# A list-scheduled attention and two-layer feed-forward kernel: new cost constants for the planner, other places for the weight rounding, six copies per pass on another engine

## The chip, the core and the metric

The kernel runs on one core of a Trainium2 chip. The metric is the device time of one execution in microseconds (us). The engines are TensorE (PE; its weight loads are shown as PEld), VectorE (DVE), ScalarE (ACT), GpSimd (POOL) and SyncE (SP, which issues most DMAs). Each engine works through its own instructions in program order, and waits for others by semaphores.

## The reference

Attention with 4 batches, 12 heads, 448 tokens and heads of 64; then two feed-forward layers on the 1792 tokens of width 768:

```python
scores = cap * np.tanh(np.matmul(q, k.transpose(0, 1, 3, 2)) * scale / cap)
attn = np.exp(scores - np.max(scores, axis=-1, keepdims=True))
attn = attn / (np.sum(attn, axis=-1, keepdims=True) + 1e-09)
x = np.matmul(attn, v)                    # then laid out as (1792, 768)
x = np.maximum(x @ w_in, 0.0) ** 2 @ w_out      # w_in 768x2048, w_out 2048x768
x = np.maximum(x @ w_in2, 0.0) ** 2 @ w_out2
```

## The kernel before

**Arithmetic.** The two feed-forward layers are computed by Strassen-Winograd products: seven products named A11, A12, S3, S2, S1, S4 and A22 instead of eight. Every fp32 operand is split into a high part (a copy to the matmul's format) and a low part (the operand minus the high part, always on VectorE), and a product takes three matmuls: high by high, high by low, low by high (lines 632 to 634).

**Stages.** Attention runs over 24 pairs of heads (`pair`). The feed-forward work runs in four passes, two for each layer, each for two batches (`layer`, `bring`, `blocks_of_g`, `stream`). A pass streams 56 chunks of weights: a chunk is six 128x128 tiles, and PE needs 18 matmuls for it. In the first 28 chunks of a pass the first product of the layer (w_in) is done, in the last 28 the second (w_out), while `blocks_of_g` makes and splits sums of the activations.

**Work on VectorE and ScalarE.** For each chunk ScalarE makes the high part of the weights (`wh`, line 284) and VectorE the low part (`wl`, line 200 through the helper `minus`; line 203 is the helper `sub`). At the start of a pass `bring` loads the twelve tiles of x of that pass, and `split_x` makes the parts of seven combinations for each of three columns c: the high part by ScalarE (line 449) or by VectorE (line 451), as its last argument says, and the low part by VectorE. Before the change S2 and A22 take VectorE, the five others ScalarE.

**Rounding of words.** The weights arrive as 64-bit words. `round_words` turns a word block into fp32: a load on SP, one ScalarE scale (line 230), three VectorE instructions (lines 233, 236, 239), and a store to DRAM on POOL's queue (line 242). `round_block` does two of them and then four sums on GpSimd (line 267), stored too. A layer has 17 blocks (8 of w_in, 9 of w_out). The buffers are few: two for words once the early blocks are done, three for the results (`wg`), a result's buffer being given back when its sums are stored.

**What sets the order.** All is written as operations with an engine, an estimated cost in ns, a place (a due time in chunks) and dependences, and `Plan.emit` orders them by a list schedule: each engine keeps a clock that the estimated costs advance. Of the first 40 waiting operations of an engine, none more than 6 places ahead of PE's next one, it takes the first that can start at the engine's clock, or else the one that can start earliest; the engine that can start first of all goes next. So the costs, the places and the engines decide the order in which each engine's queue is written; on the chip the queues then run in that order, at their own speed. `act(n)` and `dve(n, rate)` give the costs, `place` and `t0` the places. `START` is place 60.8, where pass 0 begins, and pass p begins 56 p places later.

Of the kernel before, what the change touches and what calls it, by code (L numbers as in the profile page):

```python
# [15 lines left out]
B, H, S, D = 4, 12, 448, 64  # L16
# [3 lines left out]
QW = 960  # L20
# [8 lines left out]
START = 24 * PAIR + 2  # L29
# [4 lines left out]
class Plan:  # L34
# [12 lines left out]
    def op(self, engine, cost, emit, place, deps=(), take=(), drop=(), after=()):  # L47


        self.ops.append([engine, cost, emit, place, list(deps), list(take), list(drop), None, list(after)])  # L50
        return len(self.ops) - 1
# [103 lines left out]
def pipeline(ctx: ExitStack, tc: tile.TileContext, qk, v, capt, rcap, eps, win, wout, w32, sums, x1, x2, out):  # L155
# [35 lines left out]
    op = plan.op  # L191

    def act(n, psum=False):
        return 0.833 * n + (145 if psum else 93)

    def dve(n, rate=1.04):
        return rate * n + 67

    def minus(out, a, b):
        nc.vector.tensor_tensor(out, a, b.bitcast(F32), op=ALU.subtract)  # L200
# [10 lines left out]
    def round_words(l, u, t0, ring, early):  # L211


        g, i, k = UNITS[u]
        c0, c1 = FP[k] if g else (0, HC)
        nk = 2 * (c1 - c0)
        n = nk * 128
        words = next(turns) % (3 if early else 2)
        m = {"at": [None]}

        def load():
            m["t"] = w_8[words]
            src = (wout[l][i] if g else win[l][i]).bitcast(U32).rearrange("p (h c) -> p h c", h=2)[:, :, c0 * 256:c1 * 256]
            nc.sync.dma_start(m["t"][:, :n].rearrange("p (h m) w -> p h (m w)", h=2), src)

        def scale():
            m["f"] = w_g[m["at"][0]]
            m["ff"] = m["f"].rearrange("p c m -> p (c m)")[:, :n]
            m["fu"] = m["ff"].bitcast(U32)
            nc.scalar.activation(m["ff"], m["t"][:, :n, 1].bitcast(F32), AF.Copy, scale=2.0 ** -112)  # L230

        def shift():
            nc.vector.tensor_scalar(m["fu"], m["fu"], 3, 1, op0=ALU.logical_shift_left, op1=ALU.bitwise_or)

        def lower():
            nc.vector.scalar_tensor_tensor(m["fu"], m["t"][:, :n, 0], 29, m["fu"], op0=ALU.logical_shift_right, op1=ALU.bitwise_or)  # L236

        def sign():
            nc.vector.scalar_tensor_tensor(m["fu"], m["t"][:, :n, 1], 0x80000000, m["fu"], op0=ALU.bitwise_and, op1=ALU.bitwise_or)

        def store():
            nc.gpsimd.dma_start(w32[l, g, i][:, :, c0:c1], m["f"][:, :nk].rearrange("p (h c) m -> p h c m", h=2))

        o = op("SP", n * 1024, load, t0 - 2, take=[f"ww{words}"])
        o = op("ACT", act(n), scale, t0, [o], take=[(ring, m["at"])])
        o = op("DVE", dve(n, 0.52), shift, t0, [o])
        o = op("DVE", dve(n), lower, t0, [o])
        o = op("DVE", dve(n), sign, t0, [o], drop=[f"ww{words}"])
        if words == 2:
            guard.update({(0, "c", f): [o] for f in range(4)})  # L250
        stored[l, u] = op("POOL", n * 512, store, t0, [o])
        return m

    def round_block(l, g, i, k, t0, early):


        c0, c1 = (0, HC) if g == 0 else FP[k]
        n = c1 - c0
        us = [unit_of(g, r, k) for r in (i, i + (HF if g == 0 else HC))]
        ring = "wx" if early and (i + k) % 2 == 0 else "wg"  # L260
        ms = [round_words(l, u, t0 + 2.2 * r, ring, early) for r, u in enumerate(us)]

        def one_sum(q):
            a11, a12, a21, a22 = (m["f"][:, h * n:h * n + n] for m in ms for h in range(2))
            out, a, b, how = [(a22, a21, a22, ALU.add), (a21, a11, a21, ALU.subtract),
                              (a11, a22, a11, ALU.subtract), (a12, a12, a11, ALU.subtract)][q]
            nc.gpsimd.tensor_tensor(out, a, b, op=how)  # L267

        def store():
            for r, m in enumerate(ms):  # L270
                nc.gpsimd.dma_start(sums[l, g, i][:, 2 * r:2 * r + 2, c0:c1], m["f"][:, :2 * n].rearrange("p (h c) m -> p h c m", h=2))

        o = [stored[l, u] for u in us]
        for q in range(4):
            o = [op("GP", dve(n * 128, 2.9), lambda q=q: one_sum(q), t0 + 4.5, o)]
        summed[l, g, i, k] = op("POOL", 4 * n * 128 * 512, store, t0 + 4.5, o, drop=[(ring, m["at"]) for m in ms])
        if ring == "wx":
            guard.update({(0, "d", f): [summed[l, g, i, k]] for f in range(HF)})
# [20 lines left out]
    def pair(b, j, t0, step):  # L299


        stk, pv, m = {}, {}, {}
# [23 lines left out]
        t = t0 - 3 * step  # L326
        o = op("SP", 128 * QW * 4, load_qk, t - 4, take=["raw"])
        o = op("DVE", dve(QW, 0.6), hi, t, [o], take=["qkh"])
        parts = op("DVE", dve(QW), lo, t, [o], take=["qkl"], drop=["raw"])
        v_ready = op("SP", 128 * VL * 4, load_v, t0 - 4.5, take=["vr"])  # L330

        banks = [("pv", [None]) for _ in range(2)]
        done = None
        for gi, tiles in enumerate(GROUPS):
            s, n = {"at": [None]}, len(tiles) * S
# [51 lines left out]
        def den(a):  # L387
            if a == 0:
                m["d"] = sp.tile([128, S], F32, tag="d", name="d")
            rows, of = (slice(0, 64), slice(64, 128)) if a == 0 else (slice(64, 128), slice(0, 64))  # L390
            nc.scalar.activation(m["d"][rows], pv["AB"[a]][of, :S], AF.Identity, bias=eps[of])  # L391
# [11 lines left out]
        t1 = t0 + dt[3] + 3 * step  # L403
        to = {B * NP - 2: "XY", B * NP - 1: "XZ"}.get(nth)
        back = [(to[e] if to else "pv", banks[e][1]) for e in range(2)]
        o = op("ACT", act(S), lambda: den(0), t1, [done], take=["d"])
        o = op("ACT", act(S), lambda: den(1), t1, [o])
        o = op("DVE", dve(S, 6.25), rec, t1, [o])
        o = op("DVE", dve(S), lambda: mul(0), t1, [o], drop=back[:1])
        o = op("DVE", dve(S), lambda: mul(1), t1, [o], drop=back[1:])  # L410
# [32 lines left out]
    def split_x(src, name, c, p, place, deps, on_act):  # L443

        cell = [None]

        def hi():
            if on_act:
                nc.scalar.activation(slots[cell[0]][:, 0], src(), AF.Copy)
            else:  # L450
                nc.vector.tensor_copy(slots[cell[0]][:, 0], src())

        def lo():
            minus(slots[cell[0]][:, 1], src(), slots[cell[0]][:, 0])

        o = op("ACT" if on_act else "DVE", act(S) if on_act else dve(S, 0.52), hi, place, deps, take=[("x", cell)])
        o = op("DVE", dve(S), lo, place, [o])
        x_set[p, name, c] = cell, o
        return o
# [3 lines left out]
    def bring(p, c, spots, place, t_in, free):  # L463

        l, b1 = p // 2, 2 * (p % 2)
        b2 = b1 + 1
        m = {}
        cells = [(b1, c), (b2, c), (b1, c + HC), (b2, c + HC)]

        def load():  # L470
            m["t"] = [two[n][:, i] for n, i in spots]
            for q, (b, i) in enumerate(cells):
                nc.sync.dma_start(m["t"][q], (x2 if l else x1)[b, i])

        def t2():
            m["d"] = sp.tile([128, S], F32, tag="d", name="t2") if p else two["c"][:, 5 + c]
            sub(m["d"], m["t"][3], m["t"][0])

        ring = ["d"] if p else []
        ld = op("SP", 4 * 128 * S * 4, load, t_in, [*(stored_x[l, b, i] for b, i in cells), *free])  # L480
        o1 = split_x(lambda: m["t"][0], "A11", c, p, place("A11", c), [ld], True)
        o2 = split_x(lambda: m["t"][2], "A12", c, p, place("A12", c), [ld], True)
        o = op("DVE", dve(S), lambda: sub(m["t"][0], m["t"][1], m["t"][0]), place("S3", c) - 0.2, [o1])
        o3 = op("DVE", dve(S), lambda: sub(m["t"][1], m["t"][3], m["t"][1]), place("S3", c) - 0.1, [o])
        split_x(lambda: m["t"][1], "S3", c, p, place("S3", c), [o3], True)
        o4 = op("DVE", dve(S), t2, place("S2", c) - 0.1, [o3], take=ring)
        o6 = split_x(lambda: m["d"], "S2", c, p, place("S2", c), [o4], False)
        o5 = op("DVE", dve(S), lambda: sub(m["t"][2], m["t"][2], m["d"]), place("S2", c) + 0.1, [o6, o2], drop=ring)
        o7 = split_x(lambda: m["t"][0], "S1", c, p, place("S1", c), [o], True)
        o8 = split_x(lambda: m["t"][3], "S4", c, p, place("S4", c), [ld], True)  # L490
        last = split_x(lambda: m["t"][2], "A22", c, p, place("A22", c), [o5, o7, o8], False)
        guard.update({(p, *spot): [last] for spot in [*spots, *([] if p else [("c", 5 + c)])]})

    def split_g(p, name, q, src, place, deps):
# [229 lines left out]

    blocks = [(g, f, 0) for g in range(1) for f in range(HF)] + [(1, i, k) for i in range(HC) for k in range(3)]
    for q, block in enumerate(blocks):
        round_block(0, *block, 2 + 4.7 * q, q < 11)
    for q, block in enumerate(blocks):
        round_block(1, *block, START + 32+6.4 * q, False)
    for n in range(B * NP):  # L730
        pair(*divmod(n, NP), PAIR * n, 0.65)
    op("PE", 0, open_two, START - 0.5, ready_x[-1:], drop=[("x", [NX + i]) for i in range(NY)])
# [140 lines left out]
```

## Time and profile before

| what | value |
|---|---|
| median of three runs | 1124.91 us (1124.22 to 1127.05) |
| the profiled execution | 1121.83 us, its span 1120.0 us |
| mean granted TensorE clock | 0.986 |
| PE busy, 4920 matmuls | 94% |
| DVE busy, 976 instructions | 77% |
| ACT busy, 1119 instructions | 68% |
| POOL busy, 324 instructions | 25% |

How to read it: matmuls are pipelined, so a busy PE is not PE at its peak; the number of matmuls that start in a stretch tells more. The shares are means over stages with different limits, and are read stage by stage below.

### The profile page before, as it was taken

To read this page: it belongs to the slowest core of one execution; us is meant where nothing else is said; L and a number is where in the kernel's file an instruction comes from. 1 tells how busy PE (TensorE), PEld (TensorE's weight loads), DVE (VectorE), ACT (ScalarE), POOL (GpSimd) and SP (SyncE) were. 2 spreads that over 40 slices of the span, in tenths; PEclk is the share of its full clock that TensorE was granted. 3 is DMA by queue.
4 is the path that set the end of the run, shared out by engine and by line. 5 is a ranking of instruction groups with operands and counts; after the bars stand their busy time and mean duration, and the time that the engine had idled before them with its cause. 6 is when DMAs were issued, how large, how long until landed. Compare 5 with 4: busy or idle time off the path is not lost.

```text
span 1120.0 us, 14647 instructions
## 1 busy us (share of the span) xinstructions
PE 1054.1 (94%) x4920; PEld 869.4 (78%) x4920; DVE 861.8 (77%) x976; ACT 763.3 (68%) x1119; POOL 284.0 (25%) x324
## 2 busy tenths in 40 slices
PE   6999998986999998989999889899999999999997
PEld 3444444445999897889988778799999989999996
DVE  4999898999567998985589989755886863367851
ACT  6999999884778565557775655577765556686541
POOL 0354353423223505332433333324200000000000
PEclk9999999888999999999999999999999999999999
DMA  9889899753777668767876687776446443333441
GB/s 265 295 275 314 263 292 335 238 190 116 273 231 235 224 203 295 242 239 242 279 226 209 208 312 244 224 237 227 157 138 211 152 135 99 114 100 120 131 145 58
DMA packets 107684, 237.79 MB, mean 212 GB/s; under 512 B 13648, under 2 KB 62032, under 8 KB 107600
## 3 DMA queue, kind: packets, MB, share of 16 engines
q1 hardware_dynamic: 92112, 175.42, 51.0%
q0 software_dynamic: 15488, 61.35, 14.7%
q8 instruction: 40, 0.66, 0.2%
q14 instruction: 44, 0.36, 0.1%
HBM read 169.87 MB, written 66.85 MB: 211 GB/s over the span
## 4 chain that ended last, share of the span: by engine, by line
PE 55%; DVE 14%; ACT 11%; issue 9%; DMA 6%; POOL 4%; SPq 0%; DVEq 0%; ACTq 0%; POOLq 0%
PE bank L634 16%; PE bank L632 16%; PE bank L633 16%; PE bank L362 4%; ACT bank L350 4%; DVE wl L200 3%; POOL wg L267 3%; ACT pe L354 2%; PE bank L345 2%; ACT d L391 2%; DVE xb L200 2%; DVE xc L200 2%; DMA wo<-wg 2%; DVE d L394 2%; DVE wg L236 1%
## 5 line engine op out<-in xcount | busy, mean ns | idle before, releaser
L200 DVE TENSOR_TENSOR wl<-wf,wh 128x768 fp32r<-128x768 f32 x224 | 226.7, 1014 | 147.9 <-ACT wh L284 147.3
L634 PE MATMUL bank<-xc,wl 128*128 128x448 f32 x756 | 278.9, 369 | 11.0 <-DVE wl L200 10.9
L632 PE MATMUL bank<-xc,wh 128*128 128x448 f32 x756 | 278.5, 368 | 8.8 <-ACT bank L650 3.7
L284 ACT ACTIVATE wh<-wf 128x768 fp32r<-128x768 f32 x224 | 187.7, 840 | 137.5 <-PE bank L633 105.2
L633 PE MATMUL bank<-xc,wh 128*128 128x448 f32 x762 | 280.1, 368 | 1.2 <-DVE xc L200 1.0
L632 PE MATMUL bank<-xb,wh 128*128 128x448 f32 x588 | 216.1, 368 | 7.1 <-ACT wh L284 2.4
L634 PE MATMUL bank<-xb,wl 128*128 128x448 f32 x588 | 215.5, 367 | 3.3 <-DVE wl L200 3.3
L633 PE MATMUL bank<-xb,wh 128*128 128x448 f32 x582 | 213.1, 366 | 1.7 <-DVE xb L200 1.7
L634 PEld LDWEIGHTS bank<-xc,wl 128*128 128x128 f32 x756 | 142.9, 189 | 25.9 <-DVE wl L200 14.3
L632 PEld LDWEIGHTS bank<-xc,wh 128*128 128x128 f32 x756 | 142.8, 189 | 23.5 <-ACT bank L650 4.9
L362 PE MATMUL bank<-pe,vr 128*128 128x448 f32 (+1 forms) x384 | 155.2, 586 | 1.4 <-DVE d L398 1.1
L633 PEld LDWEIGHTS bank<-xc,wh 128*128 128x128 f32 x762 | 144.0, 189 | 13.8 <-DVE xc L200 2.1
L632 PEld LDWEIGHTS bank<-xb,wh 128*128 128x128 f32 x588 | 110.7, 188 | 19.4 <-ACT wh L284 3.2
L634 PEld LDWEIGHTS bank<-xb,wl 128*128 128x128 f32 x588 | 110.6, 188 | 13.8 <-DVE wl L200 4.8
L633 PEld LDWEIGHTS bank<-xb,wh 128*128 128x128 f32 x582 | 109.6, 188 | 10.9 <-DVE xb L200 2.1
L362 PEld LDWEIGHTS bank<-pe,vr 128*128 128x128 f32 (+1 forms) x384 | 59.1, 194 | 67.7 <-issue 36.3
L350 ACT ACTIVATE bank<-bank,caps 128x896 f32<-128x896 f32 x96 | 84.2, 877 | 18.6 <-PE bank L345 18.6
L267 POOL TENSOR_TENSOR wg<-wg 128x384 f32<-128x384 f32 (+1 forms) x56 | 76.4, 1365 | 60.7 <-DMA wo<-wg 46.0
L354 ACT ACTIVATE pe<-bank,caps 128x896 f32<-128x896 f32 x96 | 87.8, 914 | 3.1
L658 ACT ACTIVATE one<-bank 128x448 f32<-128x448 f32 x88 | 47.1, 536 | 49.5 <-PE bank L634 37.0
L345 PE MATMUL bank<-qkh 64*128 64x448 f32 (+1 forms) x168 | 56.7, 573 | 23.1 <-ACT pe L354 16.4
L676 DVE TENSOR_TENSOR one<-bank,one 128x448 f32<-128x448 f32 x64 | 39.7, 620 | 44.6 <-PE bank L634 35.6
(116 smaller groups left out, 1381.9 us busy)
## 6 DMA issues: line engine op xcount, KB each, us to landing
wf<-si SPq DMA_DIRECT2D x120, 192.0 KB, 3.0
ww<-win_dram SPq DMA_DIRECT2D x27, 768.0 KB, 6.7
wf<-wi SPq DMA_DIRECT2D x96, 192.0 KB, 3.2
ww<-wout_dram SPq DMA_DIRECT2D x23, 768.0 KB, 6.5
wf<-so SPq DMA_DIRECT2D x32, 384.0 KB, 3.7
raw<-qk_dram SPq DMA_DIRECT2D x48, 240.0 KB, 5.2
wi<-wg POOLq DMA_DIRECT2D x24, 384.0 KB, 5.8
si<-wg POOLq DMA_DIRECT2D x24, 384.0 KB, 4.3
```

What stands on the lines that cost most here:

```text
L200: nc.vector.tensor_tensor(out, a, b.bitcast(F32), op=ALU.subtract)
L267: nc.gpsimd.tensor_tensor(out, a, b, op=how)
L284: nc.scalar.activation(m["hi"], m["f"], AF.Copy)
L345: nc.tensor.matmul(s["s"][:, i, :S], lhsT=k[rows, S + 128 * t:S + 128 * t + 128], rhs=q[rows, :S], start=k_low + q_low == 0, stop=k_low == 1)
L350: nc.scalar.activation(s["s"], s["s"], AF.Tanh, scale=rcap)
L354: nc.scalar.activation(s["p"][:, :k], s["s"], AF.Exp, scale=capt)
L362: nc.tensor.matmul(pv[a][:, :S], lhsT=m["v"][rows, w:w + 128], rhs=s["p"][rows, i], start=t == 0, stop=t == 3)
L632: nc.tensor.matmul(a, lhsT=hi, rhs=x(0), start=first and z == 0, stop=False, skip_group_check=more)
L633: nc.tensor.matmul(a, lhsT=hi, rhs=x(1), start=False, stop=False, skip_group_check=more)
L634: nc.tensor.matmul(a, lhsT=lo, rhs=x(0), start=False, stop=final and z == len(xs) - 1, skip_group_check=more)
L658: nc.scalar.activation(m[key], bank[:, cell[0], :S], AF.Copy)
L676: nc.vector.tensor_tensor(m[g, i, r], bank[:, cell[0], :S], m[g, i, r], op=ALU.add)
```

## The change

The cost formulas of the planner get other constants, the rounding blocks other places, and the high parts of S2 and A22 in `split_x` are made by ScalarE (`True`) and not by VectorE. No arithmetic changes.

```diff
     def act(n, psum=False):
-        return 0.833 * n + (145 if psum else 93)
-
-    def dve(n, rate=1.04):
-        return rate * n + 67
+        return 0.833 * n + 145 if psum else 0.98 * n + 105
+
+    def dve(n, rate=1.13):
+        return rate * n + 110
...
-        o = op("DVE", dve(n, 0.52), shift, t0, [o])
+        o = op("DVE", dve(n, 0.62), shift, t0, [o])
...
-            o = [op("GP", dve(n * 128, 2.9), lambda q=q: one_sum(q), t0 + 4.5, o)]
+            o = [op("GP", dve(n * 128, 2.4), lambda q=q: one_sum(q), t0 + 4.5, o)]
...
-        parts = op("DVE", dve(QW), lo, t, [o], take=["qkl"], drop=["raw"])
+        parts = op("DVE", dve(QW, 1.45), lo, t, [o], take=["qkl"], drop=["raw"])
...
-        o = op("ACT", act(S), lambda: den(0), t1, [done], take=["d"])
-        o = op("ACT", act(S), lambda: den(1), t1, [o])
+        o = op("ACT", act(S) + 80, lambda: den(0), t1, [done], take=["d"])
+        o = op("ACT", act(S) + 80, lambda: den(1), t1, [o])
...
-        o6 = split_x(lambda: m["d"], "S2", c, p, place("S2", c), [o4], False)
+        o6 = split_x(lambda: m["d"], "S2", c, p, place("S2", c), [o4], True)
...
-        last = split_x(lambda: m["t"][2], "A22", c, p, place("A22", c), [o5, o7, o8], False)
+        last = split_x(lambda: m["t"][2], "A22", c, p, place("A22", c), [o5, o7, o8], True)
...
     for q, block in enumerate(blocks):
-        round_block(0, *block, 2 + 4.7 * q, q < 11)
+        round_block(0, *block, 2 + 4.6 * q, q < 11)
     for q, block in enumerate(blocks):
-        round_block(1, *block, START + 32+6.4 * q, False)
+        round_block(1, *block, START + 24+7 * q, False)
```

## Rows read from the trace of the kernel before

**Rows 1.** The page, part 1: busy us, share, instructions.

```profile
PE 1054.1 (94%) x4920; PEld 869.4 (78%) x4920; DVE 861.8 (77%) x976; ACT 763.3 (68%) x1119; POOL 284.0 (25%) x324
```

**Rows 2.** Windows: stretch and its length, each engine's busy us (instructions), clock, DMA.

```profile
245.00:280.00 35.00, 25.32 (x103) 19.13 (x103) 34.29 (x42) 16.84 (x29) 13.74 (x15) 0.90 0.50 168
...
280.00:340.00 60.00, 60.00 (x298) 55.60 (x297) 34.14 (x45) 45.02 (x77) 15.53 (x20) 1.00 0.77 252
...
340.00:500.00 160.00, 151.36 (x719) 136.16 (x717) 145.69 (x169) 99.40 (x149) 61.20 (x58) 0.98 0.73 241
...
575.00:730.00 155.00, 140.79 (x677) 125.89 (x676) 144.60 (x168) 89.75 (x136) 56.03 (x61) 1.00 0.73 238
...
730.00:1000.00 270.00, 269.38 (x1330) 249.29 (x1329) 167.87 (x208) 177.86 (x284) 27.68 (x30) 1.00 0.50 159
```

**Rows 3.** Waits of PE in 245:280, 340:500, 575:730: us in total, times, longest.

```profile
PE bank L634 <- DVE wl L200: 5.0, 1, 5.0
...
PE bank L634 <- DVE wl L200: 3.4, 3, 2.2
...
PE bank L634 <- DVE wl L200: 5.9, 5, 1.9
```

**Rows 4.** Timeline near 228 us: start, length, instruction, [idle before, releaser].

```profile
225.25 0.58 ACT L449 ACTIVATE xb<-gb 128x448 fp32r<-128x448 f32 x1 [1.73 <-DVE gb L203]
...
228.98 0.74 PE L345 MATMUL bank<-qkh 64*128 64x448 f32 x2 [3.35 <-ACT pe L354]
```

**Rows 5.** Timeline near 272 us.

```profile
270.61 0.39 DVE L451 CAST xc<-gb 128x448 fp32r<-128x448 f32 x1
...
271.57 0.95 DVE L200 TENSOR_TENSOR wl<-wf,wh 128x768 fp32r<-128x768 f32 x1
...
272.58 0.74 PE L634 MATMUL bank<-xc,wl 128*128 128x448 f32 x1 [5.00 <-DVE wl L200]
```

**Rows 6.** Timeline near 490 us and near 658 us.

```profile
489.82 0.48 PE L634 MATMUL bank<-xc,wl 128*128 128x448 f32 x1 [2.22 <-DVE wl L200]
...
657.13 0.54 ACT L658 ACTIVATE one<-bank 128x448 f32<-128x448 f32 x1 [6.78 <-DVE y L704]
...
658.46 0.47 PE L632 MATMUL bank<-xb,wh 128*128 128x448 f32 x1 [2.20 <-ACT wh L284]
```

**Rows 7.** Windows of stretches at the low clock, columns as in Rows 2.

```profile
227.40:234.20 6.80, 5.22 (x12) 2.94 (x13) 6.59 (x8) 6.67 (x9) 0.59 (x1) 0.52 0.78 267
268.40:275.20 6.80, 2.62 (x7) 2.15 (x7) 6.70 (x11) 0.00 (x0) 3.09 (x3) 0.52 0.53 177
...
490.20:493.60 3.40, 3.40 (x12) 3.02 (x11) 2.80 (x4) 1.11 (x2) 0.13 (x1) 0.54 1.01 399
```

**Rows 8.** Groups by line: count, busy us, mean ns, idle before.

```profile
L200 DVE TENSOR_TENSOR wl<-wf,wh 128x768 fp32r<-128x768 f32 x224 | 226.7, 1014 | 147.9 <-ACT wh L284 147.3
...
L236 DVE SCALAR_TENSOR_TENSOR wg<-ww,wg 128x768 uint32<-128x768 uint32 (+1 forms) x53 | 50.9, 961 | 1.7
...
L200 DVE TENSOR_TENSOR qkl<-raw,qkh 128x960 fp32r<-128x960 f32 x24 | 35.8, 1494 | 0.8
L233 DVE TENSOR_SCALAR wg<-wg 128x768 uint32<-128x768 uint32 (+1 forms) x56 | 31.9, 569 | 6.1 <-ACT wg L230 6.1
```

**Rows 9.** Lines 451 and 449: count, ns min/median/max, first and last start.

```profile
L451 DVE CAST xc<-gb x6: 383/386/1194, 270.6 to 910.9; 128x448 fp32r<-128x448 f32 x6
...
L449 ACT ACTIVATE xc<-gb x20: 560/562/582, 260.9 to 905.7; 128x448 fp32r<-128x448 f32 x20
```

**Rows 10.** Timeline near 421 us and near 442 us.

```profile
420.88 9.45 POOL L267 TENSOR_TENSOR wg<-wg 128x384 f32<-128x384 f32 x1 [6.30 <-DMA wi<-wg]
...
441.25 0.93 ACT L230 ACTIVATE wg<-ww 128x768 f32<-128x768 f32 x1 [0.72 <-DMA si<-wg]
...
442.95 0.74 PE L632 MATMUL bank<-xc,wh 128*128 128x448 f32 x1 [2.40 <-ACT wh L284]
```

**Rows 11.** Sums on GpSimd, and the tile wo from 740 us on.

```profile
L267 POOL TENSOR_TENSOR wg<-wg x56: 736/1024/9449, 56.7 to 794.4; 128x384 f32<-128x384 f32 x46, 128x256 f32<-128x256 f32 x10
...
L595 SPq DMA_DIRECT2D wf<-wo x12: 319/320/493, 783.1 to 813.8; - x12
L242 POOL DMA_DIRECT2D wo<-wg x5: 682/687/691, 748.9 to 787.9; - x5
```

## The prediction

> **What bounds the kernel now.** First the page: PE is busy 94% of the span, and no other engine over 77% [rows 1]. That is a mean, so next the windows by stage [rows 2]. From 280 to 340 us and from 730 to 1000 us PE has no gap worth naming: 1330 matmuls in 269.38 us, 0.2025 us each, and a chunk of 18 takes 3.65 us. That is one place of the planner in the feed-forward part, and no order of VectorE's work makes it shorter. In three other stretches PE falls short: it is idle 35.00 - 25.32 = 9.7 us from 245 to 280, 8.6 us from 340 to 500, 14.2 us from 575 to 730, together 32.5 us. In each of them DVE is busy 91 to 98% (34.29 of 35, 145.69 of 160, 144.60 of 155), against 57% from 280 to 340. These are the end of attention with the first x parts, and the second halves of passes 0 and 1 with the start of the pass behind each, while weights of a layer are still rounded. From 730 us on, with the last word stored at 787.9 [rows 11], nothing of this is left.
>
> Third, who releases PE there: most often the low part of the weights on VectorE, 5.0, 3.4 and 5.9 us [rows 3]. Single stalls in the timelines show how. At 271.57 us the `wl` that PE waits for starts only after a run of x parts in VectorE's queue; PE stood 5.00 us [rows 5]. At 657.13 a ScalarE copy had waited 6.78 us for a VectorE result, the `wh` behind it came late, and PE stood 2.20 us [rows 6]. At 225.25 ScalarE waited 1.73 us for a VectorE difference, with attention's tanh and exp behind it, and PE stood 3.35 us [rows 4]. These are faults of order: an engine stands at the head of its queue for something that the plan thought done.
>
> Fourth, after the longest stalls the clock is down: it is granted at 0.52 in 227.4 to 234.2 and 268.4 to 275.2, and at 0.54 in 490.2 to 493.6 [rows 7], which is the lower of the levels 1.2 and 2.4 GHz nearly throughout. Work done there takes twice as long, so half of the busy time is lost: 2.6, 1.3 and 1.7 us, together 5.6 us.
>
> **The change part by part.** The plan's own time counts for nothing on the chip; what changes is the order.
>
> *Costs.* For 768 columns `dve` goes from 1.04 x 768 + 67 = 866 ns to 978; the rows have 1014 for `wl` and 961 for line 236. The shift goes from 466 to 586 ns, measured 569. The low part of q and k goes from 1065 to 1502, measured 1494 [rows 8]. So the old plan took VectorE for 10 to 29% faster than it is, and put work on other engines behind VectorE results that were not there yet. One constant goes the other way: a sum on GpSimd from 2.9 x 384 + 67 = 1181 ns to 1032, at the measured median of 1024, but with no room for the longest one of 9449 [rows 11]. What can be had from VectorE's order: the stalls of 3.35, 5.00, 2.22 and 2.20 us [rows 4 to 6], 12.8 us; the lost clock behind three of them, 5.6 us; and the other waits for `wl` after 340 us, 3.4 - 2.2 + 5.9 = 7.1 us [rows 3]. Together 25.5 us. All of it is the one end. The other is a loss: a list schedule that avoids one stall can make another, and it can lose as much as the largest one, 5.0 + 1.3 us, in each of the three stretches [rows 2, 5, 7], 19 us. I take half of 25.5 less what the casts below account for, 2.5: a gain of 11.5 us. Half, because DVE stays over 90% loaded there: a perfect order still needs the work to fit.
>
> *Copies.* Gone from VectorE are 24 casts (three c, two names, four passes) in seven groups of which one stands in [rows 9], at 386 ns: 9.3 us and a little for the slow ones. They come back as 24 copies on ScalarE of 562 ns [rows 9], 13.5 us on an engine that is 48 to 62% busy in these stretches. Only those ahead of a stall of PE count: five before the one at 272.58 and one before that at 489.82, each some 0.42 us with its gap, 2.5 us; this is the value that I take. All eighteen of the three loaded starts would be 18 x 0.42 = 7.6 us, the one end. The other: the low part now waits for a copy that is 0.18 us longer, 18 x 0.18 = 3.2 us lost. The six of pass 3 are free either way, since PE is full there.
>
> The wait that this adds is on ScalarE: the copy for S2 waits for a VectorE difference, that for A22 for VectorE's difference and low parts. Queued behind it are the `wh` copies, for them `wl`, and for that PE.
>
> *Places.* Layer 0's blocks move forward by 0.1 place each, at most 1.6 places, 5.8 us. Layer 1's first block moves 8 places forward (29 us), the 14th all but stays, the last moves 1.6 back. Counting places, the second halves of passes 0 and 1 hold blocks at 32, 38.4, 44.8, 51.2 and 89.6 to 108.8 before, and at 31, 38, 45, 52 and 87, 94, 101, 108 after: four and four both times. A block is 2 x (0.569 + 2 x 0.961) = 5.0 us of VectorE [rows 8]. I value this at nothing, between a gain and a loss of one block, 5.0 us. The cover is the slack from 280 to 340, where DVE is idle 26 us. If it is gone, a block falls into a full stretch for 5.0 us. The word loads move on SP's queue with their blocks and can hold the `wf` loads behind them; with PE full there at a DMA share of 0.77 [rows 2] I see no cost. The last block ends later: its store at 787.9 would come at 793.7. The fetches of `wo` run from 783.1 to 813.8 [rows 11], and this block, the last columns of the last row, is among the later ones; if PE waited for it, 5.8 us is the price, and I take none.
>
> *A rule weighed.* One of GpSimd's sums lasts 9.45 us where the median is 1.02 [rows 10, 11], while VectorE's queue runs without gaps. Its buffer comes late, ScalarE's scale at 441.25 waits for its store, the next `wh` is late, and PE stands 2.40 us [rows 10]. The Trainium skill (SBUF — State Buffer, § SBUF: two separate sides) says that VectorE instructions with two SBUF inputs and GpSimd take a shared port pair as an exclusive lock, and that the loser waits for the whole instruction. The trace agrees. By that rule no mean cost, old or new, tells the plan when such a sum ends, and the rounding's part of the stalls stays: this is the second rival below.
>
> **Sum.** Order -11.5, copies -2.5, places 0: -14.0 us. The profiled execution, 1121.83 us (span 1120.0 and 1.83 around it), would become 1107.8. It lies 3.08 us under the median of the runs; from the median, 1124.91 - 14.0 = 1110.9 us.
>
> **Rivals.** *ScalarE's queue head becomes the late one (slower).* At each loaded start of a pass (0, 1, 2) a new copy holds ScalarE for VectorE as in [rows 4]: 3.35 us idle and 2.6 us of clock, 6.0 us. Three of them are 18 us, less 2.5 for the casts, with no gain of order: 1124.9 + 15.5 = 1140.4 us. With half the order's gain it is about 1135. It decides from the point where the copy holds ScalarE longer than PE has chunks prepared, about one chunk, 3.65 us. For it: the same kind of copy did this at 225.25, and ScalarE waited 6.78 us at 657.13. Against it: the new plan knows VectorE's durations, and ScalarE has idle time.
>
> *Hardly any change.* The misjudged moments are not in the means but in GpSimd's lock and the few buffers [rows 10], and the order gains nothing: only the casts, 1124.9 - 2.5 = 1122.4 us. For it: two of the single stalls end with ScalarE, not VectorE. Against it: `wl` releases PE in all three stretches.
>
> *The stretches come nearly clean (faster still).* All idle time of the three, 32.5 us, and all the clock of [rows 7], 5.6 us, and the 3.35 us of [rows 4] are 41.5 us; seven tenths would be 29 us, 1096 us. For it: DVE itself is idle 25.4 us in the three [rows 2], not far from PE's 32.5. Against it: 91 to 98% busy leaves little room to reorder.
>
> **How the numbers follow.** Forecast 0.54, its own range 1100 to 1121 (a gain of 4 to 25 us); the cleaner one 0.11; hardly any change 0.15; ScalarE's queue 0.20. A measurement of this kernel can tell about 0.3%, 3.4 us, from no change. So faster 0.65, same 0.15, slower 0.20. The range runs from 1096, where half of the cleaner case is left out, to 1133, which takes in the milder half of the slower one and a block in a full stretch.
>
> **What would show it.** Right: no casts on line 451 and 84 copies on line 449; PE's idle time in the three stretches down from 32.5 to about 20 us, the waits for `wl` shorter, the low-clock stretches at 268 and 490 gone; full speed from the second half of pass 2 on, as before. Wrong: new rows of ScalarE's line 449 waiting for line 203 or 200 with PE idle behind them; the same idle time in other places; DVE over 95% in a stretch that holds more rounding than before; PE waiting for `wf` near 800 us.

## The result, and the profile after

The changed kernel takes 1114.61 us (median of 7 runs, 1109.72 to 1119.58) against 1124.90 us (7 runs, 1123.44 to 1128.71): a ratio of 0.9903, 95% interval 0.9874 to 0.9931, so 10.3 us less where 14.0 were forecast. (The ratio goes by the means of the runs and makes 10.9 us of 1125; the medians differ by 10.3.) The profiled execution took 1114.6 us, 7.2 us less than the profiled one of the kernel before.

The page after, its span, busy time and granted clock:

```profile
span 1112.8 us, 14612 instructions
...
PE 1052.8 (95%) x4920; PEld 870.7 (78%) x4920; DVE 858.7 (77%) x952; ACT 777.9 (70%) x1143; POOL 282.7 (25%) x324
...
PEclk9999999999999998899999999999999999999999
```

VectorE has 24 instructions fewer and ScalarE 24 more than in [rows 1]: line 451 has none left, and line 449 has 84 copies. VectorE's busy time falls by only 3.1 us. Where the time went is in the windows by stage, beside [rows 2]:

```profile
245.00:280.00 35.00, 25.69 (x113) 21.55 (x112) 31.42 (x41) 21.09 (x38) 11.59 (x14) 0.95 0.62 208
...
280.00:340.00 60.00, 59.38 (x294) 54.63 (x293) 33.14 (x43) 43.91 (x75) 19.87 (x24) 1.00 0.75 246
...
340.00:500.00 160.00, 151.84 (x709) 136.69 (x708) 148.01 (x167) 100.28 (x151) 64.01 (x60) 0.96 0.74 246
...
575.00:730.00 155.00, 149.75 (x719) 135.32 (x718) 138.27 (x160) 99.10 (x149) 48.52 (x55) 0.99 0.73 235
...
730.00:1000.00 270.00, 267.59 (x1319) 247.32 (x1319) 171.32 (x205) 182.69 (x290) 21.66 (x23) 1.00 0.47 149
```

From 575 to 730 us PE starts 719 matmuls and not 677: 42 x 0.2025 = 8.5 us, more than the 7.2 us between the two profiled executions. From 245 to 280 it is ten more, 2 us; from 340 to 500 ten fewer and from 730 to 1000 eleven fewer, some 2 us lost in each. From 340 to 500 PE is idle a little less than before (8.2 us for 8.6) and starts fewer all the same: the granted clock is 0.96 there and was 0.98. PE's idle time in the three loaded stretches is 9.3 + 8.2 + 5.3 = 22.7 us, where it was 32.5.

The rounding moved between these stretches as well. Each word block takes line 236 once, and a rounding block is two word blocks. VectorE's time on line 236 alone, before:

```profile
340.00:500.00 160.00, 11.37 (x11) 0.98 0.73 241
575.00:730.00 155.00, 10.41 (x12) 1.00 0.73 238
```

and after:

```profile
340.00:500.00 160.00, 13.82 (x13) 0.96 0.74 246
575.00:730.00 155.00, 8.50 (x10) 0.99 0.73 235
```

So the stretch that gained has one rounding block less, and the one that lost has one more.

Who releases PE there, for the three stretches in turn (total us, times, longest), answers [rows 3]:

```profile
PE bank L634 <- DVE wl L200: 7.0, 2, 5.7
PE bank L632 <- ACT bank L650: 1.7, 2, 1.1
...
PE bank L634 <- DVE wl L200: 7.2, 5, 2.8
...
PE bank L634 <- DVE wl L200: 3.9, 2, 2.7
PE bank L632 <- ACT bank L650: 0.6, 1, 0.6
```

The waits for `wl` did not shrink: 18.1 us, against 14.3. What went are waits in which ScalarE was late. By the whole list of each stretch, ScalarE releases PE for 4.1 us after and for 14.2 us before. What ScalarE itself waited for stands in the groups of ScalarE's instructions from 575 to 730 us, with what ended the idle time before them. First the kernel before, the groups that waited for VectorE:

```profile
L658 ACT ACTIVATE one<-bank 128x448 f32<-128x448 f32 x12 | 6.4, 530 | 7.9 <-DVE y L704 6.8 <-PE bank L634 1.1
L498 ACT ACTIVATE xc<-t2g 128x896 fp32r<-128x896 f32 x4 | 3.7, 944 | 4.4 <-DVE t2g L203 4.4
...
L498 ACT ACTIVATE xb<-gb 128x896 fp32r<-128x896 f32 x3 | 2.8, 949 | 9.3 <-DVE gb L203 9.3
```

and the same stretch after:

```profile
L658 ACT ACTIVATE one<-bank 128x448 f32<-128x448 f32 x13 | 7.0, 539 | 6.3 <-PE bank L634 4.1 <-DVE y L704 2.0
L498 ACT ACTIVATE xc<-t2g 128x896 fp32r<-128x896 f32 x4 | 3.8, 945 | 2.2 <-DVE t2g L203 2.1
...
L449 ACT ACTIVATE xc<-t 128x448 fp32r<-128x448 f32 x3 | 1.7, 580 | 2.9 <-DVE t L203 2.8
```

The 6.78 us wait of [rows 6] is in the first line before; after, that group waits 2.0 us for VectorE. With all groups ScalarE stood for VectorE 27.9 us before and 13.4 us after; how much of that is the constants is taken up below. The new copies are among the waiters (last line), and PE waits for none of them in this stretch.

The largest stall stayed where it was. The timeline after, at the end of attention, is the counterpart of [rows 5], with no cast ahead of `wl`:

```profile
263.26 1.42 DVE L200 TENSOR_TENSOR xc<-gb,xc 128x448 fp32r<-128x448 f32 x1
...
264.28 1.25 POOL L267 TENSOR_TENSOR wg<-wg,wg 128x384 f32<-128x384 f32 x1
264.61 1.75 DVE L200 TENSOR_TENSOR wl<-wf,wh 128x768 fp32r<-128x768 f32 x1
...
266.41 0.74 PE L634 MATMUL bank<-xc,wl 128*128 128x448 f32 x1 [5.68 <-DVE wl L200]
```

`wl` still comes behind x parts, and lasts 1.75 us, with a sum on GpSimd beside it, where it took 0.95 in [rows 5].

### The profile page after: what moved, and what is told of

Same layout as the page of the kernel before. It is cut to its first block, busy times and chain, and to the rows that moved or that the text cites. A ratio compares the mean times of both kernels' runs of the same rounds, so it can differ in the third digit from the quotient of the medians.

```text
span 1112.8 us, 14612 instructions
## 1 busy us (share of the span) xinstructions
PE 1052.8 (95%) x4920; PEld 870.7 (78%) x4920; DVE 858.7 (77%) x952; ACT 777.9 (70%) x1143; POOL 282.7 (25%) x324
## 3 DMA queue, kind: packets, MB, share of 16 engines
q0 software_dynamic: 15488, 61.35, 15.1%
## 4 chain that ended last, share of the span: by engine, by line
PE 66%; DVE 11%; ACT 7%; issue 7%; DMA 5%; POOL 3%; SPq 0%; DVEq 0%; POOLq 0%; ACTq 0%
PE bank L634 21%; PE bank L632 20%; PE bank L633 20%; PE bank L362 3%; ACT bank L350 3%; POOL wg L267 2%; DVE d L394 2%; ACT d L391 2%; PE bank L345 2%; ACT pe L354 2%; DVE xc L200 2%; DVE wl L200 1%; DMA wo<-wg 1%; DVE wg L236 1%; DMA si<-gd 1%
## 5 line engine op out<-in xcount | busy, mean ns | idle before, releaser
L200 DVE TENSOR_TENSOR wl<-wf,wh 128x768 fp32r<-128x768 f32 x224 | 221.7, 995 | 126.0 <-ACT wh L284 124.8
L362 PE MATMUL bank<-pe,vr 128*128 128x448 f32 (+1 forms) x384 | 151.3, 575 | 4.4 <-issue 1.6
L350 ACT ACTIVATE bank<-bank,caps 128x896 f32<-128x896 f32 x96 | 84.2, 877 | 14.2 <-PE bank L345 14.2
```

Source lines behind the costliest of these rows:

```text
L350: nc.scalar.activation(s["s"], s["s"], AF.Tanh, scale=rcap)
L362: nc.tensor.matmul(pv[a][:, :S], lhsT=m["v"][rows, w:w + 128], rhs=s["p"][rows, i], start=t == 0, stop=t == 3)
```

## The experiments

The kernel before was run beside each group of runs, and its own median moved from 1123 to 1127 us between the chips, so ratios are compared, and differences are given in us of 1125.

**The three parts one by one.** The diffs are the three groups of the change: the constants (`act`, `dve`, the rates, `+ 80`), the two `True`, the two lines of places.

> Only the planner's cost constants change; copies and places stay as before. Theory A (the order written with truer costs brings most of the gain of 10.3 us): 1113 to 1118 us, PE idle from 575 to 730 us down from 14.2 to under 8 us. Theory B (the places bring it, since one rounding block leaves the second half of pass 1): 1122 to 1127 us. Theory C (a reshuffle: any change of order moves the time by several us either way, and the parts do not add up): anywhere from 1112 to 1130 us, and not in line with the parts' sum.

> Only the high parts of S2 and A22 go to ScalarE, with the old costs and places. Theory A: a gain of about 2.5 us (0 to 7.6), 1122 us. Theory B: the same. The rival on ScalarE's queue head: slower, 1130 to 1140 us, with ScalarE's line 449 waiting for VectorE ahead of a stall of PE.

> Only the places of the rounding blocks change. Theory A: no change, 1120 to 1130 us (a block of 5.0 us either way). Theory B (places): 1114 to 1119 us, with the gain from 575 to 730 us, where 10 words are rounded and not 12, and no gain from 340 to 500 us.

**Two of the three.**

> The change without its places. Adding the single parts so far (costs -3.8 us, copies -8.2 us of some 1127) gives -12.0 us, a ratio of 0.989. If the places, which alone cost 3.8 us, cost the same beside the other two, this kernel is faster than the whole change (0.9903), at 0.987; if the truer costs put the places right, it is at 0.990 or above. If parts don't add up since each reshuffles the order: between 0.985 and 0.998.

> The change without the copies. By adding: -3.8 + 3.8 = 0, a ratio of 1.000, and the copies are the whole of the gain. If the copies are worth only 2.5 us in the changed kernel, as predicted: 0.9925. If copies are worth 6 to 8 us there too: 0.996 to 0.998.

> The change with the old cost constants. By adding: -8.2 + 3.8 = -4.4 us, a ratio of 0.996. If the costs are worth 11.5 us as predicted once the places move: 1.000. If the costs matter little: 0.991 to 0.993.

What was measured, with the kernel before as 1:

| constants | copies | places | ratio | 95% interval | us of 1125 |
|---|---|---|---|---|---|
| new | | | 0.9966 | 0.9950 to 0.9981 | -3.8 |
| | new | | 0.9927 | 0.9904 to 0.9951 | -8.2 |
| | | new | 1.0034 | 1.0014 to 1.0053 | +3.8 |
| new | new | | 0.9960 | 0.9935 to 0.9984 | -4.5 |
| new | | new | 0.9921 | 0.9893 to 0.9949 | -8.9 |
| | new | new | 0.9993 | 0.9973 to 1.0012 | -0.8 |
| new | new | new | 0.9903 | 0.9874 to 0.9931 | -10.9 |

The parts do not add up. Two pairs show it: constants and copies give -4.5 for a sum of -12.0, and constants and places give -8.9 for a sum of 0, each a miss of over 7 us with an interval of +-4.2. The third pair (-0.8 for -4.4) and all three (-10.9 for -8.2) miss by less than their intervals. The constants bring 3.8 us alone, bring 12.7 (+-3.9) beside the places, and beside the copies lose 3.7 (+-3.9), which can't be told from nothing. The places cost 3.8 alone and 7.4 (+-3.5) beside the copies, and bring 6.4 (+-4.3) beside both others. The copies bring 8.2 alone and 2.0 (+-4.5) as the last of the three. (The +- join the two half intervals as the root of the sum of squares.) Of the theories, B falls, since the places alone lose; A holds only beside the new places; C describes the table, but its 1112 to 1130 us left room for nearly any result. The expectation for the constants was also wrong in its number from 575 to 730 us: PE is idle 155 - 143.34 = 11.7 us there, not under 8.

With the places alone the loss is at the end of attention: in the timeline of that kernel PE waits 8.72 us there, where it was 5.00. From 245 to 280 us it starts 87 matmuls and not 103.

```profile
276.66 0.74 PE L634 MATMUL bank<-xc,wl 128*128 128x448 f32 x1 [8.72 <-DVE wl L200]
```

**The copies in an unchanged order.** The plan of before is kept, and only the engine that gets the instruction differs; PE, POOL and SP have the very instructions of before in the same order.

```diff
-            if on_act:
+            if True:
                 nc.scalar.activation(slots[cell[0]][:, 0], src(), AF.Copy)
```

> The plan before, so the very order of before, but the 24 copies are issued on ScalarE at the spot in the program where the casts of VectorE stood. This tells the engine's effect from that of a new order. If the casts' time on VectorE counts: 1118 to 1123 us, stalls at 272 and 490 us shorter by about 2 and 0.4 us. If ScalarE's queue head decides, since the plan did not foresee these copies there: 1127 to 1140 us.

Measured: ratio 0.9947, interval 0.9929 to 0.9965, -6.0 us (-8.0 to -3.9). The two stalls that the expectation named, in the timeline of that kernel:

```profile
270.00 0.74 PE L634 MATMUL bank<-xc,wl 128*128 128x448 f32 x1 [4.14 <-DVE wl L200]
...
489.79 0.47 PE L634 MATMUL bank<-xc,wl 128*128 128x448 f32 x1 [1.36 <-DVE wl L200]
```

They are 0.9 us shorter each, for 2 and 0.4 expected. What line 449 waited for there (us, times) shows that ScalarE's queue head did come to stand:

```profile
  DVE t L203: 11.4, 6
  DVE gb L203: 6.8, 5
```

18.2 us of waiting for VectorE, where it was 6.8 in the kernel before, and the kernel is faster all the same. The rival on ScalarE's queue falls.

**Without the sums on GpSimd.** Two kernels, the one before and the changed one, with their 136 sums left out (the stores stay, so the layer's results are other numbers); the plan and the order are kept.

```diff
+            if q == 4:
-            nc.gpsimd.tensor_tensor(out, a, b, op=how)
+                nc.gpsimd.tensor_tensor(out, a, b, op=how)
```

> The kernel before in its very order, without the 136 sums on GpSimd (their results are left out, the stores stay). It tells what the sums and their sharing with VectorE cost. If the lock is a large part of the stalls, as the second rival had it: 15 us or more faster, 0.986 or less, the low parts of the weights at 0.95 us throughout instead of 1.08 from 340 to 500 us, and the stall near 442 us gone. If it is a small part: 0.995 to 1.0, with VectorE still over 85% busy in the loaded stretches.

Measured: 0.9703 (0.9675 to 0.9731), 33.4 us faster. Its page:

```profile
PE 1043.3 (96%) x4920; PEld 866.8 (80%) x4920; DVE 810.8 (75%) x976; ACT 762.1 (70%) x1119; POOL 110.6 (10%) x188
```

Its windows of the two long loaded stretches:

```profile
340.00:500.00 160.00, 158.10 (x779) 145.85 (x778) 138.74 (x178) 105.53 (x160) 19.86 (x36) 1.00 0.77 262
...
575.00:730.00 155.00, 153.38 (x748) 139.72 (x747) 126.75 (x168) 99.33 (x153) 25.55 (x40) 1.00 0.81 269
```

Its group of `wl` (the line of `wh` is one higher by the edit):

```profile
L200 DVE TENSOR_TENSOR wl<-wf,wh 128x768 fp32r<-128x768 f32 x224 | 213.6, 955 | 154.6 <-ACT wh L285 153.7
```

VectorE runs the same 976 instructions in 810.8 us and not 861.8 [rows 1], `wl` in 955 ns and not 1014 [rows 8]. PE is idle 1.9 and 1.6 us in the two stretches, where it was 8.6 and 14.2 [rows 2], with 12 and 13 word blocks rounded there, no fewer than before. VectorE is still 87 and 82% busy there, and that is no loss.

To tell the reading of SBUF from a buffer that is merely held longer, each sum was replaced by two fills of its output, which read nothing:

```diff
-            nc.gpsimd.tensor_tensor(out, a, b, op=how)
+            nc.gpsimd.memset(out, 0.0)
+            nc.gpsimd.memset(out, 1.0)
```

> The kernel before in its order, with two fills by a constant on GpSimd in place of each sum (the sums are left out, the stores stay): GpSimd still works and still holds the buffers, but reads nothing from SBUF. If the sums cost 33 us because they and VectorE's two-input instructions keep each other out: as fast as without sums, 0.97 to 0.975. If they cost it because the buffer is given back later: near the kernel before, 0.99 to 1.0, in proportion to the time that the fills take against 1.2 us for a sum.

Measured: 0.9700 (0.9659 to 0.9740). A line of its page and two of its groups:

```profile
PE 1043.0 (96%) x4920; PEld 866.8 (80%) x4920; DVE 811.4 (75%) x976; ACT 761.7 (70%) x1119; POOL 216.8 (20%) x460
...
L200 DVE TENSOR_TENSOR wl<-wf,wh 128x768 fp32r<-128x768 f32 x224 | 213.2, 953 | 154.5 <-ACT wh L285 153.7
...
L267 POOL MEMSET wg<- 128x384 f32 (+1 forms) x112 | 46.2, 413 | 58.4 <-DMA wo<-wg 43.3 <-DMA wi<-wg 15.0
```

Two fills take some 0.8 us, two thirds of a sum (171 us for 136 sums, 1.26 each), and cost nothing that can be measured against no sums at all; VectorE is busy 811.4 us beside them. So it is what the sums do to VectorE's instructions, and these to them, not GpSimd's time; the fills do hold the buffers some 0.4 us less a sum, so a small share of the other cause is not excluded. The Trainium skill's rule of the shared port pair (SBUF — State Buffer, § SBUF: two separate sides) limits the lock against two-input VectorE instructions to GpSimd work that reads SBUF; this pair of kernels agrees, with VectorE busy 811.4 us beside the fills, 810.8 without sums and 861.8 beside the sums.

> The changed kernel in its order, without the 136 sums on GpSimd (results left out, stores kept). It tells whether the change and the sums' conflict draw on the same stalls. If the new order pays by absorbing what the sums do to VectorE: no faster than the kernel before without sums, 0.968 to 0.973. If the two are separate (order and copies save their 11 us on top of 34): 0.958 to 0.963.

Measured: 0.9750 (0.9730 to 0.9769). Without the sums the changed kernel is not faster than the kernel before without them (0.9703), if anything slower. The change and the sums draw on the same stalls. That the new order pays by fitting itself around the sums is one reading; the other, that without them VectorE has so much room that no order is left to gain, fits as well (PE is idle 1.9 and 1.6 us in the two long stretches), and no run here tells them apart.

**Other places.** First layer 0's line put back to `2 + 4.7 * q`, all else as changed:

> The changed kernel with layer 0's blocks back at 4.7 places, layer 1's new places kept; it splits the places' part, which brought some 6 us beside the new costs (0.9903 against 0.996) though alone it cost 3.8 us. If layer 1's places bring it (one block fewer in the second half of pass 1): 0.990 still. If layer 0's bring it (at the end of attention): 0.996.

Measured: 0.9940 (0.9914 to 0.9966). It lies between the two answers, and its interval overlaps those of both kernels, so of the whole time it stays open which layer's places matter. The stretch from 575 to 730 us tells more. First without any new places (constants and copies alone), then with layer 1's:

```profile
575.00:730.00 155.00, 144.51 (x678) 131.14 (x677) 140.87 (x162) 95.63 (x145) 60.69 (x63) 0.96 0.76 253
...
575.00:730.00 155.00, 149.84 (x727) 136.99 (x726) 141.92 (x162) 101.85 (x154) 50.34 (x57) 0.99 0.73 236
```

Line 236 runs 13 times there in the first and 11 times in the second. So the gain of that stretch comes with layer 1's places and goes without them; the other parts alone start 678 matmuls, as the kernel before does (677). It needs the constants as well: copies and places with the old ones start 688. From 340 to 500 us the second starts only 698.

Then layer 1's blocks by hand:

```diff
-        round_block(1, *block, START + 24+7 * q, False)
+        round_block(1, *block, START + [30, 40, 50, 56.5, 61.5, 66.5, 71.5, 76.5, 81.5, 90, 98, 106, 111.5, 117, 122.5, 128, 133.5][q], False)
```

> The changed kernel with layer 1's rounding blocks at places picked by hand: 3 in place of 4 in each second half of passes 0 and 1, the rest in the first halves of passes 1 and 2 where VectorE is 57 to 65% busy. Theory: each block that leaves a loaded stretch takes 5.0 us of VectorE and four sums out of it, so two blocks give 5 to 10 us against the change, a ratio of 0.982 to 0.986 to the kernel before. Rival (the reshuffle of the whole order, or buffers too few for blocks 5 places apart): 0.988 to 1.0.

Measured: 1110.68 us, 0.9855 (0.9829 to 0.9882), as expected: 1.4% better than before, and by its middle 5 us better than the change, with intervals that just overlap. Its windows of the two long stretches:

```profile
340.00:500.00 160.00, 157.81 (x769) 145.12 (x768) 144.27 (x167) 108.53 (x165) 46.29 (x52) 0.99 0.74 243
...
575.00:730.00 155.00, 146.38 (x692) 132.63 (x691) 137.06 (x158) 93.96 (x144) 56.39 (x61) 0.97 0.75 248
```

POOL is busy 46 us and not 64 from 340 to 500, and PE starts 769 matmuls and not 709; from 575 to 730, where POOL is busy 56 and not 49 us, it starts 692 and not 719. Line 236 runs 11 times and not 13 in the first stretch, 12 and not 10 in the second: against the change the loss follows the rounding, and the total came as expected although the second stretch, for which the theory had a gain too, lost. It is not the rounding alone: the kernel before also has 11 and 12 there and starts only 719 and 677.

## Why the prediction was right, and where it was not

*What bounds the kernel* was read rightly from 245 us on: the three loaded stretches lose the time, the rest runs at PE's pace, and the gain came from one of them. Left out was attention ahead of them, where PE is idle 24.9 us before and 26.5 after. The forecast of about 20 us of PE's idle time left there met 22.7.

*The order* was priced at -11.5 us. Given the other two parts the constants brought 0.9993 - 0.9903 = 0.0090, 10.1 us (+-3.9), so the size holds for the change as it was made. Alone they bring 3.8, and beside the copies nothing that can be told from zero. The mechanism is half right. The stall at 658 us and its kind went, ScalarE waiting for VectorE results that the plan took for done. And it is the constants that did it: from 575 to 730 us ScalarE stands for VectorE 9.1 to 15.1 us in the six kernels here that have the new constants and the sums, and 22.9 to 34.4 us in the five that have the old ones. But there that alone gives PE nothing: with the constants alone ScalarE stands 9.1 us and PE starts 673 matmuls, with 7.2 us of waiting for `wl`; with the places too it starts 700, and with all three parts 719. The waits for `wl`, on which the sum also leaned, grew from 14.3 to 18.1 us, and the stall near 272 us is still there, with 5.68 us. Of the clock, the low stretch at 490 us is gone, that at 268 is half as long (265.6 to 269.0), and there are new ones near 419, 464 and 672 us:

```profile
265.60:269.00 3.40, 2.59 (x7) 2.34 (x8) 3.40 (x4) 0.00 (x0) 3.02 (x4) 0.54 0.96 346
419.20:426.00 6.80, 5.81 (x16) 5.17 (x17) 6.80 (x9) 5.47 (x7) 2.73 (x1) 0.52 0.84 268
463.60:470.40 6.80, 5.72 (x15) 5.12 (x16) 6.80 (x12) 3.29 (x6) 0.54 (x1) 0.52 0.79 267
671.80:675.20 3.40, 2.71 (x7) 2.45 (x8) 3.40 (x6) 1.11 (x2) 0.58 (x1) 0.54 0.91 293
```

Each goes with a wait for `wl` (5.68, 2.82, 2.21 and 2.68 us), as those at 268 and 490 us did before. From 340 to 500 us that is 13.6 us at the low clock, where it was 6.9 before, which goes with the ten matmuls lost there at no more idle time.

*The copies* were priced at -2.5 us, counting only the casts that stood ahead of one of two stalls. In an unchanged order they bring 6.0, near the end of 7.6 that counts all eighteen of the loaded starts. With VectorE over 90% busy in these stretches, the casts counted here also where no visible stall stood behind them. As the last part of the change they bring 2.0 (+-4.5), which can't tell 2.5 from 6.

*The places* were priced at nothing, by counting blocks by their places in the second halves of two passes, four and four. The trace does not bear the count out for the stretches that lose time, which reach beyond those halves: there are 12 word blocks before and 10 after from 575 to 730 us, and 11 and 13 from 340 to 500. Alone the places cost 3.8 us, at the end of attention; beside the constants and the copies they bring 6.4 (+-4.3), and the gain from 575 to 730 hangs on them. The step that fails is the sum itself. It adds three terms as if each had one value, and each part here reorders all queues. That the total came within 4 us of the measured change is in part luck: each as the last of the three, the parts are worth 10.1, 2.0 and 6.4 us, which is not 10.9 either, and one of them had been put at nothing.

*The rivals.* ScalarE's queue head stood for VectorE, 16 us in the changed kernel for line 449 and 18 us in the kernel with the unchanged order, where it was 6.8, and PE's matmuls waited for that line once, 0.8 us, in the changed kernel. Hardly any change, because of GpSimd's sums: its premise was far larger than thought, 33.4 us hang on the sums, and its conclusion was wrong, since the constants brought 10.1 us beside the other two parts with the sums in place. That the gain vanishes without the sums ties it to them; how the new order avoids them is not shown.

## What to carry to other kernels

In a kernel ordered by a list schedule, price an edit of costs, places or engines as one reordering, and measure the parts in each other's company before keeping or dropping one: here the same edit was worth +7 or -6 us. Where an engine is over 90% busy, work taken off it can count also where no visible stall stands behind it: 24 casts of 0.39 us gave 6.0 us here, where the six ahead of stalls had been priced at 2.5. And count what a stretch holds in the trace, not by its places in the plan. Before tuning an order around a slow engine, look at whether its instructions last longer beside another engine's: leaving out GpSimd's sums showed more than twice the gain that any order found.

## What was not expected of the hardware

136 sums on GpSimd, 171 us of its time, lengthened VectorE's same 976 instructions by 51 us, from 810.8 to 861.8, and the kernel by 33 us. Fills of the same tiles cost neither (VectorE 811.4 us, ratio 0.9700). One sum took 9.45 us for 1.02, from 420.88 to 430.33 us. VectorE ran nine two-input instructions of 0.95 to 1.08 us meanwhile, without a gap until 429.45. So as far as the trace tells, the sum stood through a row of instructions, not through one, as the rule weighed in the prediction would have it.
